# First two token tiles of a linear-attention and GEGLU block: order of loads, low words and products changed

## The chip, the cores and the metric

The kernel runs on one core of one Trainium2 chip. The metric is the device time of one execution in microseconds (us). The engines are named as in the profile: PE is TensorE (matrix products and transposes), DVE is VectorE, ACT is ScalarE, POOL is GpSimd, and SP is SyncE, whose queue issues the DMAs.

## The reference

2048 tokens of 576 features go through a layer norm; two branches read the result, and their product is added to the input. All arrays are float32.

```python
def _A_ref(x, wqkv, wo):                       # linear attention, 32 heads of 18
    qkv = ...(x @ wqkv).reshape(B, S, 3, H, Dh)
    phi = lambda t: jnp.where(t > 0, t + 1, jnp.exp(t)) + 1e-6
    pq, pk = phi(q), phi(k)
    kv = jnp.einsum("bhsd,bhse->bhde", pk, v)
    z = jnp.einsum("bhsd->bhd", pk)
    num = jnp.einsum("bhqd,bhde->bhqe", pq, kv)
    den = jnp.einsum("bhqd,bhd->bhq", pq, z)[..., None] + 1e-6
    return (num / den) ... @ wo

def _B_ref(x, w_gate, w_up, w_down):           # GEGLU
    h = gelu(x @ w_gate) * (x @ w_up)
    return h @ w_down

xn = _layernorm(x)
return x + _A_ref(xn, A_wqkv, A_wo) * silu(_B_ref(xn, ...))
```

## The kernel before

The 2048 tokens are cut into 16 tiles of 128. The first stage, the only one that the change touches, takes each tile through the layer norm and multiplies it with the k and v columns of `wqkv` (with a last group of q columns beside them). Later stages (the other q columns, the attention output, the gate, up and down matrices) take most of the 1500 us and are the same in both kernels.

**Words.** A float32 operand is used as two words: a high word, which is a copy into the type fp32r, and a low word, the difference of the source and the high word. Each product of x and W is seven passes over pairs of words (`KV_PASSES`, pairs of W word and x word). For one half j of the 576 features, x has a tile `xo` of five slots: 0 and 1 are the high words of two chunks of 128 features, 2 is a mixed slot that holds the last 32 features in several copies, partly as low words, and 3 and 4 are the low words of chunks 0 and 1. W has the same five slots. Pass (0, 3) needs x's low words, (3, 0) needs W's, and (2, 2) needs the mixed slot of both. `x_mm(t, c)` makes the product of tile t with column group c (0, 1, 2: 384, 384 and 448 columns), two halves of seven passes, 14 products in one PSUM bank.

**Preparing x.** `load_x` loads a tile, `spread` makes its mean and variance on DVE (two BN statistics, one aggregate) and the inverse root on ACT (Ln, Exp), `scales` mends it in three small DVE instructions, and `center` subtracts the mean and scales in place (one DVE instruction of 128x768). `turn` transposes the tile on PE in six pieces into two PSUM banks, three for each half j; `place` copies the high words out of PSUM (ACT, L85) and subtracts for the low words (DVE, two instructions a half: 128x256, and 32x128 for the mixed slot); `save` copies the float32 values out for later (ACT).

**Preparing W.** `load_kv(c, j)` loads one of six parts, `kv_hi` copies its high words (ACT), and `kv_lo(c, j, eng)` subtracts for its low words on the engine it is given: one instruction of 128x768 (896 for group 2) and one of 32x384 (448) for the mixed slot. Before, `kv_lo(0, 0)`, `kv_lo(1, 0)` and `kv_lo(2, 0)` run on DVE and `kv_lo(0, 1)`, `kv_lo(1, 1)`, `kv_lo(2, 1)` on POOL.

**After the products.** `k_post` applies phi to the k columns (two DVE instructions out of PSUM, Exp on ACT, an addition on POOL), `v_post` copies the v columns (ACT), `q_post` does phi for the q columns, ending with two POOL additions into `w_q`, and `kv_mm(t)` multiplies k with v into two PSUM banks. `q_turn` transposes `w_q` into a free corner of the x transposes' banks. `make_masks` fills constants with seven POOL instructions; they are read only after all tiles.

**Order.** Nearly every instruction is pinned to the program's order on its engine, and each engine works through its list in order; semaphores tie the engines together. The order of the first tiles is written out by hand at the end of `block_kernel`, from L1066 on: 22 transposes of a constant (`idle`, L1067) first, then the loads on SP's queue, then the preparations and products of tiles 0 to 2. From tile 3 on a loop calls `kv_tile`. The line numbers 85, 88, 91, 94 and 97 are the helpers that record each ACT, DVE, product, POOL and DMA instruction; L168 is the transpose in `turn`, L402 the one in `q_turn`. Transposed tiles 1 and later, and the product banks, share six PSUM banks (`bank`); tile 0's transposes use two others (`own_bank`).

Of the kernel before, what the change touches and what calls it, by code (L numbers as in the profile page):

```python
# [10 lines left out]
AF = mybir.ActivationFunctionType  # L11
# [42 lines left out]
def block_kernel(ctx, tc, x, xe, wq_d, wkv0_d, wkv1_d, wkv2_d, wo, wgu_d, wd_d, out):  # L54
# [6 lines left out]
    def bank(name):  # L61
        return ps.tile([P, 512], F32, tag="one", bufs=6, name=name)
# [21 lines left out]
    def act(*args, **kw):  # L84
        pin(nc.scalar.activation(*args, **kw))  # L85
# [4 lines left out]
    def mm(*args, **kw):  # L90
        pin(nc.tensor.matmul(*args, **kw))  # L91

    def pool(op, *args, **kw):
        pin(getattr(nc.gpsimd, op)(*args, **kw))  # L94
# [21 lines left out]
    def load_x(n, k):  # L116

        if n % 2 == 0:
            xstat[n // 2] = big(14 + n // 2 % 2, [P, 2, 2, 3 * P], F32, f"x_{n}")
        dma(  # L120
            out=xstat[n // 2][:, n % 2 : n % 2 + k],
            in_=xe[n * P : (n + k) * P].rearrange("(t p) j d -> p t j d", p=P),
        )
# [31 lines left out]
    def center(n):  # L155

        xs = xstat[n // 2][:, n % 2]
        m, r = scale_of.pop(n)
        vec("tensor_scalar", xs, xs, m, r, op0=ALU.subtract, op1=ALU.mult)

    def turn(n, new=bank):

        xs = xstat[n // 2][:, n % 2]
        tiles = [new(f"xt_{n}_{j}") for j in range(2)]
        xts[n] = [t[:, 0 : 3 * P].rearrange("p (k t) -> p k t", k=3) for t in tiles]
        for j in range(2):
            for k in range(3):
                pin(nc.tensor.transpose(xts[n][j][:, k, :], xs[:, j, k * P : (k + 1) * P], ident))  # L168
        q_turn([t for t in sorted(pqt) if t < n - 1], [(t, 3) for t in tiles])

    def place(n, js=(0, 1), words=(0, 1)):

# [16 lines left out]
    def save(n):  # L189

        tb, t = divmod(n, TT)
        s, b = divmod(tb, 2)
        for j, nm in enumerate(BS[b]):
            if t == 0:
                at_ = XM[s][nm]
                xf[s][nm] = (mid if at_ < 3 else big)(at_, [P, 3, TBN], F32, f"xf_{s}_{nm}")
            act(xf[s][nm][:, :, t * P : (t + 1) * P], xts[n][j], AF.Copy)
        xts.pop(n)

    mom, scale_of, xts = {}, {}, {}  # L200

    def to_operand(o, src, c):
        act(o[:, 0:3, c], src[:, :, c], AF.Copy)
# [15 lines left out]
    def keep(s, nm, o):  # L219
        d = dr.tile([P, 5, TBN], F32, name=f"kept_{s}_{nm}")  # L220
        dma(out=d, in_=o.bitcast(F32))
        store[s, nm] = d
# [24 lines left out]
    def kv_part(c, j, i):  # L247
        n = KV.index((c, j))
        if n < 5:
            return kv_parts(n, i, i + 1)[:, 0]  # L250
        w = 5 * CW[KV[i][0]]
        return wkv[i][:, w : w + CW[2]]
# [3 lines left out]
    def load_kv(c, j):  # L256
        n = KV.index((c, j))
        if n % 2 == 0:
            raws["kv", n // 2] = big((2, 3, 12)[n // 2], [P, 2, 3, CW[c]], F32, f"rw_{n}")
        raws[c, j] = raws["kv", n // 2][:, n % 2]  # L260
        dma(out=raws[c, j], in_=wkv_d[c][j])

    def kv_hi(c, j):
        n = KV.index((c, j))
        if n < 5:
            act(kv_parts(n, 0, 3), raws[c, j], AF.Copy)
        else:
            for i in range(3):
                act(kv_part(c, j, i), raws[c, j][:, i, :], AF.Copy)

    def kv_lo(c, j, eng, mixed=(False, True)):

        n, raw, r = KV.index((c, j)), raws[c, j], slice(2 * KR, 3 * KR)
        if False in mixed:
            if n < 5:
                eng("tensor_sub", kv_parts(n, 3, 5), raw[:, 0:2, :], kv_parts(n, 0, 2).bitcast(F32))
            else:
                for i in range(2):
                    eng(
                        "tensor_sub", kv_part(c, j, 3 + i), raw[:, i, :],  # L280
                        kv_part(c, j, i).bitcast(F32),
                    )
        if True in mixed:
            o = kv_part(c, j, 2)[r]
            eng("tensor_sub", o, raw[r, 2, :], o.bitcast(F32))
# [49 lines left out]


    KV_PASSES = [(0, 0), (1, 1), (3, 0), (4, 1), (0, 3), (1, 4), (2, 2)]
    pkv, pks, vas, es, pqt, pqx, ph4, ph, ph_d = ({} for _ in range(9))

    def x_mm(t, c):  # L340

        tb, i = divmod(t, TT)
        s, b = divmod(tb, 2)
        pkv[t, c] = o = bank(f"kv_{t}_{c}")
        for j in range(2):
            for n, (wi, xi) in enumerate(KV_PASSES):
                mm(
                    o[:, 0 : CW[c]], xo[s][BS[b][j]][:, xi, i * P : (i + 1) * P], kv_part(c, j, wi),
                    start=(j == 0 and n == 0), stop=(j == 1 and n == len(KV_PASSES) - 1),
                )  # L350

    def k_post(t, c):

# [13 lines left out]
    def v_post(t, c):  # L367

        if c == 1:
            vas[t] = slot([P, NHG, P], F32, f"va_{t}")  # L370
            pool("memset", vas[t][:, :, 0:1], 1.0)
        va, src = vas[t], pkv[t, c]
        n = 2 * TW - D
        if c == 1:
            src = src[:, TW - n : TW]
            act(va[:, 0, 1 : GW + 1], src[:, 0:GW], AF.Copy)
            act(va[:, 1, 1 : n - GW + 1], src[:, GW:n], AF.Copy)
        else:
            a = 2 * GW - n
            act(va[:, 1, n - GW + 1 : GW + 1], src[:, 0:a], AF.Copy)  # L380
            act(
                va[:, 2:4, 1 : GW + 1],
                src[:, a : a + 2 * GW].rearrange("p (g j) -> p g j", g=2), AF.Copy,
            )
            act(va[:, 4, 1 : W4 + 1], src[:, a + 2 * GW : TW], AF.Copy)

    def q_post(t):

        w = tmp([P, 4, Q4], f"w_q{t}")
        src, o, e = pkv[t, 2][:, TW : CW[2]], w[:, 2], w[:, 3]  # L390
        vec("tensor_scalar", e, src, 0.0, None, op0=ALU.min)
        vec("tensor_scalar", o, src, 0.0, EPS, op0=ALU.max, op1=ALU.add)
        act(e, e, AF.Exp)
        for i in range(2):
            pool("tensor_add", w[:, i], o, e)
        pqt[t] = w[:, 0:2]

    def q_turn(ts, banks):

        for t, (b, i) in zip(ts, banks):  # L400
            o = b[:, i * P : (i + 1) * P]
            pin(nc.tensor.transpose(o, pqt.pop(t), ident))  # L402
            pqx[t] = o

    def q_keep():
# [14 lines left out]
    def kv_tile(t, mid_=(), end=(), after=()):  # L420

        ahead = t % (2 * TT) != 2 * TT - 1
        x_mm(t, 0)
        if ahead:
            turn(t + 1)
        k_post(t, 0)
        x_mm(t, 1)
        if ahead:
            place(t + 1)
            save(t + 1)  # L430
        run(list(mid_))
        k_post(t, 1)
        v_post(t, 1)
        x_mm(t, 2)
        if t - 1 in vas:
            kv_mm(t - 1)
        run(list(end))
        v_post(t, 2)
        q_post(t)
        run(list(after))  # L440

# [625 lines left out]
        pin(nc.tensor.transpose(first[i % 2][:, 0:P], ident, ident))  # L1067
    load_x(0, 1)
    load_kv(0, 0)
    load_kv(0, 1)  # L1070
    load_x(1, 1)
    load_kv(1, 0)
    load_kv(1, 1)
    load_x(2, 1)
# [6 lines left out]
    center(0)  # L1081
    turn(0, own_bank)
    kv_hi(0, 0)
    kv_lo(0, 0, vec, (False,))
    place(0, (0,))
    kv_lo(0, 0, vec, (True,))
    kv_hi(0, 1)
    kv_lo(0, 1, pool)
    place(0, (1,), (0,))
    spread(1, 1)  # L1090
    kv_hi(1, 0)
    place(0, (1,), (1,))
    x_mm(0, 0)
    scales(1)
    center(1)
    kv_lo(1, 0, vec, (False,))
    kv_hi(1, 1)
    kv_lo(1, 1, pool)
    turn(1)
    place(1)  # L1100
    kv_lo(1, 0, vec, (True,))
    load_x(4, 2)
    x_mm(1, 0)
    kv_hi(2, 0)
    spread(2, 2)
    kv_lo(2, 0, vec)
    x_mm(0, 1)
    kv_hi(2, 1)
    kv_lo(2, 1, pool)
    save(0)  # L1110
    save(1)
    k_post(0, 0)
    x_mm(1, 1)
    scales(2)
    center(2)
    k_post(1, 0)
# [2 lines left out]
    x_mm(0, 2)  # L1119
    turn(2)  # L1120
    place(2)
    k_post(1, 1)
    v_post(1, 1)
    x_mm(1, 2)
    save(2)
    q_post(0)
    v_post(0, 2)
    center(3)
    q_post(1)
    v_post(1, 2)  # L1130
    make_masks()

    def x_next(n):

# [4 lines left out]


    x_mm(2, 0)
    kv_mm(0)
    turn(3)
    k_post(2, 0)
    x_mm(2, 1)
    place(3)
# [5 lines left out]
    kv_mm(1)  # L1152
    x_next(4)
    v_post(2, 2)
    q_post(2)
    load_q(0)
    for n in range(3, 2 * TT):
        ends = []
        if n < 2 * TT - 2:
            ends.append(lambda n=n: x_next(n + 2))  # L1160
        if n >= TT:
            j, c = divmod(n - TT, 2)
            prep_q(c, j)
            if n == TT + 1:
                load_q(1)
        if n == 2 * TT - 1:
            ends += [lambda i=i: difference(0, i) for i in range(3)]
        kv_tile(n, end=ends)
        if n in (4, 6):
            load_x(n + 4, 2)  # L1170
        if n == TT:
            for nm in BS[0]:
                keep(0, nm, xo[0][nm])
        if n == TT + 3:
            keep(0, "B22", xo[0]["B22"])

# [162 lines left out]
```

## Time and profile before

| | |
|---|---|
| median of 3 runs | 1501.02 us (1500.9 to 1503.89) |
| the profiled execution: its time | 1501.39 us |
| its span in the trace | 1499.7 us |
| PE busy in the span | 1489.9 us, 99% |
| DVE, ACT, POOL busy | 1063.7, 562.1, 537.2 us |
| tiles 0 to 3 (span 0 to 41.3 us) | the only part of the program with a changed order |

Times inside the trace count from the start of the span. A row of the timeline gives the start, the time to the last end, the engine, the line, the operation, output and inputs, the shape, the number of instructions merged, and in brackets the idle time before it with what ended that. A row of the table by windows gives, for each stretch, the busy time of each engine, the granted TensorE clock (1.00 is full), the busy share of the DMA engines and the GB/s they moved. Busy PE is modelled from pipelined products, so losses on PE are better read from the starts of its products.

### The profile page before, as it was taken

What the parts mean: (1) busy time and instruction counts of PE and PEld (TensorE: products, weight loads), DVE (VectorE), ACT (ScalarE), POOL (GpSimd) and SP (SyncE); (2) the same over time, 40 slices, a digit from 0 to 9 for tenths busy, and PEclk for the clock granted to TensorE, in tenths of its full rate; (3) what the DMA queues carried; (4) which work ended last, traced back from release to release, by engine and by line L of the source; (5) the groups of instructions that cost most, each with busy time, mean ns of one, the idle gap of its engine ahead of it and who ended that gap; (6) DMA issues with size and microseconds to landing.
All of it is one profiled execution on the core that took longest, in us unless ns stands there. A gap on an engine that the chain in (4) does not pass through costs nothing.

```text
span 1499.7 us, 22460 instructions
## 1 busy us (share of the span) xinstructions
PE 1489.9 (99%) x8390; PEld 1330.9 (89%) x8390; DVE 1063.7 (71%) x1604; ACT 562.1 (37%) x1047; POOL 537.2 (36%) x519
## 2 busy tenths in 40 slices
PE   8999999999999999999999999999999999999998
PEld 7989989988888888888888888888899999999998
DVE  7576476467887877788877788787785466555766
ACT  5435345333322233232232232222445454444443
POOL 4342340135655545655544665544410020000120
PEclk9999999999999999999999999999999999999999
DMA  4423204544444333443423443423688766786873
GB/s 185 142 119 136 83 3 182 182 189 157 172 155 152 120 128 134 172 173 135 152 106 128 167 172 146 160 111 128 213 321 264 232 211 227 232 283 226 292 253 116
DMA packets 112215, 257.15 MB, mean 171 GB/s; under 512 B 10138, under 2 KB 38682, under 8 KB 110058
## 3 DMA queue, kind: packets, MB, share of 16 engines
q1 hardware_dynamic: 110474, 246.80, 46.3%
q0 software_dynamic: 1632, 8.91, 1.6%
q8 instruction: 66, 1.08, 0.3%
q14 instruction: 43, 0.35, 0.1%
HBM read 157.73 MB, written 97.91 MB: 170 GB/s over the span
## 4 chain that ended last, share of the span: by engine, by line
PE 97%; DVE 1%; DMA 0%; POOL 0%; ACT 0%; issue 0%; SPq 0%; POOLq 0%; ACTq 0%
PE bd L952 26%; PE al L746 15%; PE de L746 15%; PE ga L746 15%; PE kv L91 8%; PE be L746 8%; PE s L91 4%; PE q L91 3%; PE kv_a L91 1%; PE xt L168 1%; DMA tr<-in_wd_dram 0%; PE idle L1067 0%; PE d L91 0%; PE kw L91 0%; PE b L91 0%
## 5 line engine op out<-in xcount | busy, mean ns | idle before, releaser
L952 PE MATMUL bd<-t,s 128*128 128x288 f32 x3024 | 401.3, 295 | 0.2 <-DVE u L88 0.2
L952 PEld LDWEIGHTS bd<-t,s 128*128 128x128 f32 x3024 | 400.9, 188 | 0.6 <-DVE u L88 0.5
L88 DVE TENSOR_TENSOR s<-sr,s 128x512 fp32r<-128x512 f32 x252 | 176.0, 738 | 120.0 <-ACT s L85 112.9
L85 ACT ACTIVATE s<-sr 128x512 fp32r<-128x512 f32 x252 | 148.9, 625 | 189.0 <-PE bd L952 128.1
L94 POOL TENSOR_TENSOR hs<-h,h 128x512 f32<-128x512 f32 x68 | 94.7, 1402 | 201.8 <-DVE h L88 199.1
L85 ACT ACTIVATE h<-h 128x512 f32<-128x512 f32 x108 | 67.0, 633 | 244.7 <-POOL sm L94 124.3
L94 POOL TENSOR_TENSOR sx<-sx 128x288 f32<-128x288 f32 x24 | 27.9, 1181 | 322.9 <-DVE sx L88 321.8
L91 PE MATMUL kv<-wkv,xo_B 128*128 128x384 f32 (+1 forms) x672 | 133.3, 353 | 1.3 <-POOL wkv L94 0.9
L91 PEld LDWEIGHTS kv<-wkv,xo_B 128*128 128x128 f32 x672 | 120.0, 190 | 6.8 <-POOL wkv L94 1.6
L88 DVE TENSOR_TENSOR wa<-raw,wa 128x256 fp32r<-128x256 f32 x72 | 81.2, 1128 | 49.6 <-ACT wa L85 46.4
L94 POOL TENSOR_TENSOR sm<-raw 128x384 f32<-128x384 f32 x72 | 75.7, 1051 | 110.3 <-DMA raw<-in_wgu_dram 70.8
L88 DVE TENSOR_TENSOR h<-h,u 128x512 f32<-128x512 f32 x108 | 95.7, 886 | 3.7
L85 ACT ACTIVATE wa<-sm 128x1152 fp32r<-128x1152 f32 x36 | 41.8, 1161 | 136.8 <-PE de L746 136.8
L88 DVE TENSOR_TENSOR wa<-sm,wa 128x768 fp32r<-128x768 f32 x72 | 63.4, 881 | 36.9 <-ACT wa L85 36.1
L94 POOL TENSOR_TENSOR td<-td 128x288 f32<-128x288 f32 x72 | 71.3, 991 | 50.6 <-DMA td<-in_wd_dram 46.4
L88 DVE TENSOR_TENSOR wb<-raw,wb 128x256 fp32r<-128x256 f32 (+1 forms) x108 | 72.4, 671 | 7.5 <-ACT wb L85 6.0
L88 DVE TENSOR_TENSOR wb<-sm,wb 128x256 fp32r<-128x256 f32 x72 | 60.9, 845 | 20.6 <-ACT wb L85 20.0
L85 ACT ACTIVATE u<-al 128x512 f32<-128x512 f32 x72 | 40.9, 592 | 88.1 <-PE al L746 88.1
L746 PE MATMUL al<-xo_B,wa 128*128 128x512 f32 x252 | 63.0, 389 | 0.0
L746 PE MATMUL al<-xr_B,wa 128*128 128x512 f32 x252 | 63.0, 389 | 0.0
L746 PE MATMUL be<-xo_T,wa 128*128 128x512 f32 x252 | 63.0, 389 | 0.0
L746 PE MATMUL be<-xr_T,wa 128*128 128x512 f32 x252 | 63.0, 389 | 0.0
(168 smaller groups left out, 2763.4 us busy)
## 6 DMA issues: line engine op xcount, KB each, us to landing
sr<-hs SPq DMA_DIRECT2D x252, 256.0 KB
hs<-h SPq DMA_DIRECT2D x68, 512.0 KB
raw<-in_wgu_dram SPq DMA_DIRECT2D x36, 768.0 KB
hs<-hs SPq DMA_DIRECT2D x102, 256.0 KB
td<-in_wd_dram SPq DMA_DIRECT2D x18, 576.0 KB
td<-td SPq DMA_DIRECT2D x18, 576.0 KB
tr<-td SPq DMA_DIRECT2D x16, 576.0 KB
tr<-in_wd_dram SPq DMA_DIRECT2D x12, 576.0 KB
```

The source lines that it names most:

```text
L85: pin(nc.scalar.activation(*args, **kw))
L88: pin(getattr(nc.vector, op)(*args, **kw))
L91: pin(nc.tensor.matmul(*args, **kw))
L94: pin(getattr(nc.gpsimd, op)(*args, **kw))
L168: pin(nc.tensor.transpose(xts[n][j][:, k, :], xs[:, j, k * P : (k + 1) * P], ident))
L746: nc.tensor.matmul(o, w[0:rows, wi, :], xop[0:rows, xi, :], start=(start and n == 0), stop=(n == len(PASSES) - 1), skip_group_check=True,)
L952: nc.tensor.matmul(banks[j][:, 0:HALF], hw[n, s][:, a, t * P : (t + 1) * P], w[:, c, g % 4], start=(new and g == 0 and m == 0), stop=(g == ...
```

## The change

Six things change, all in the first tiles:

- On SP's queue tile 1's load moves ahead of the second part of W's group 0.
- `kv_lo(0, 0)` moves from DVE to POOL. POOL then makes three of the first four parts' low words; `kv_lo(1, 0)` stays on DVE and is one piece, behind tile 1's low words.
- Tile 1's statistics and centring stand ahead of W's second part on ACT and DVE; tile 1's transposes stand in the midst of tile 0's first product.
- `x_mm` takes a list of passes, so that the products with W's high words (`HI`) of both tiles run first, and those with its low words (`LO`) and the mixed slots (`MIX`) of the second half come behind them, in turn for tiles 0 and 1.
- `q_post` is parted: its DVE instructions (`q_parts`) come earlier in the hand-written order. Tile 3's transposes stand ahead of `kv_mm(0)`, and only tile 0's `w_q` is transposed there; tile 1's follows with tile 2's, one tile later.
- `make_masks` is called after tile 5 in the loop.

```diff
-    def turn(n, new=bank):
+    def turn(n, new=bank, q=True):
...
-        q_turn([t for t in sorted(pqt) if t < n - 1], [(t, 3) for t in tiles])
+        if q:
+            q_turn([t for t in sorted(pqt) if t < n - 1], [(t, 3) for t in tiles])
+        else:
+            xtb[n] = tiles
...
     KV_PASSES = [(0, 0), (1, 1), (3, 0), (4, 1), (0, 3), (1, 4), (2, 2)]
+    HI, LO, MIX = [(0, 0), (1, 1), (0, 3), (1, 4)], [(3, 0), (4, 1)], [(2, 2)]
+    def of(*jp):
+        return [(j, p) for j, ps_ in jp for p in ps_]
...
-    def x_mm(t, c):
+    def x_mm(t, c, passes=None):
...
+        for j, (wi, xi) in passes or [(j, p) for j in range(2) for p in KV_PASSES]:
+            n = left[t, c] = left[t, c] - 1
+            mm(
+                pkv[t, c][:, 0 : CW[c]], xo[s][BS[b][j]][:, xi, i * P : (i + 1) * P],
+                kv_part(c, j, wi), start=(n == 2 * len(KV_PASSES) - 1), stop=(n == 0),
+            )
...
     load_kv(0, 0)
+    load_x(1, 1)
     load_kv(0, 1)
-    load_x(1, 1)
...
     kv_hi(0, 0)
-    kv_lo(0, 0, vec, (False,))
-    place(0, (0,))
-    kv_lo(0, 0, vec, (True,))
-    kv_hi(0, 1)
-    kv_lo(0, 1, pool)
-    place(0, (1,), (0,))
+    kv_lo(0, 0, pool)
+    place(0, (0, 1), (0,))
     spread(1, 1)
-    kv_hi(1, 0)
-    place(0, (1,), (1,))
-    x_mm(0, 0)
+    place(0, (0,), (1,))
     scales(1)
     center(1)
-    kv_lo(1, 0, vec, (False,))
+    kv_hi(0, 1)
+    x_mm(0, 0, of((0, HI), (0, LO), (0, MIX), (1, HI[:2])))
+    place(0, (1,), (1,))
+    kv_lo(0, 1, pool)
+    turn(1)
+    place(1, (0, 1), (0,))
+    x_mm(0, 0, of((1, HI[2:])))
+    kv_hi(1, 0)
+    place(1, (0, 1), (1,))
+    x_mm(1, 0, of((0, HI[:2]), (0, LO), (1, HI[:2]), (0, HI[2:]), (0, MIX), (1, HI[2:])))
+    kv_lo(1, 0, vec)
     kv_hi(1, 1)
     kv_lo(1, 1, pool)
-    turn(1)
-    place(1)
-    kv_lo(1, 0, vec, (True,))
+    x_mm(0, 0, of((1, LO), (1, MIX)))
+    x_mm(1, 0, of((1, LO), (1, MIX)))
     load_x(4, 2)
-    x_mm(1, 0)
+    x_mm(0, 1, of((0, HI), (0, LO), (0, MIX), (1, HI)))
+    x_mm(1, 1, of((0, HI), (0, LO), (0, MIX), (1, HI)))
     kv_hi(2, 0)
+    save(1)
     spread(2, 2)
     kv_lo(2, 0, vec)
-    x_mm(0, 1)
+    x_mm(0, 1, of((1, LO), (1, MIX)))
     kv_hi(2, 1)
     kv_lo(2, 1, pool)
     save(0)
-    save(1)
     k_post(0, 0)
-    x_mm(1, 1)
+    x_mm(1, 1, of((1, LO), (1, MIX)))
...
-    make_masks()
...
     x_mm(2, 0)
+    turn(3, q=False)
     kv_mm(0)
-    turn(3)
+    q_turn((0,), [(xtb.pop(3)[0], 3)])
...
+        if n == TT + 1:
+            make_masks()
```

More of the change, by code (lines that the diff above doesn't have):

```diff
@@ L193, in save @@
         for j, nm in enumerate(BS[b]):
-            if t == 0:
+            if nm not in xf[s]:
                 at_ = XM[s][nm]
@@ L198, in save @@
         xts.pop(n)
-    mom, scale_of, xts = {}, {}, {}
+    mom, scale_of, xts, xtb = {}, {}, {}, {}
     def to_operand(o, src, c):
@@ L337, in block_kernel @@
     KV_PASSES = [(0, 0), (1, 1), (3, 0), (4, 1), (0, 3), (1, 4), (2, 2)]
+    HI, LO, MIX = [(0, 0), (1, 1), (0, 3), (1, 4)], [(3, 0), (4, 1)], [(2, 2)]
+    def of(*jp):
+        return [(j, p) for j, ps_ in jp for p in ps_]
+    left = {}
     pkv, pks, vas, es, pqt, pqx, ph4, ph, ph_d = ({} for _ in range(9))
-    def x_mm(t, c):
+    def x_mm(t, c, passes=None):
         tb, i = divmod(t, TT)
         s, b = divmod(tb, 2)
[L344 to L350, printed above, removed]
+        if (t, c) not in pkv:
+            pkv[t, c] = bank(f"kv_{t}_{c}")
+            left[t, c] = 2 * len(KV_PASSES)
+        for j, (wi, xi) in passes or [(j, p) for j in range(2) for p in KV_PASSES]:
[4 more added lines that the diff above has]
+            )
     def k_post(t, c):
@@ L385, in v_post, with q_parts @@
             act(va[:, 4, 1 : W4 + 1], src[:, a + 2 * GW : TW], AF.Copy)
-    def q_post(t):
+    def q_parts(t):
         w = tmp([P, 4, Q4], f"w_q{t}")
@@ L392, in q_post @@
         vec("tensor_scalar", o, src, 0.0, EPS, op0=ALU.max, op1=ALU.add)
-        act(e, e, AF.Exp)
+        pqt[t] = w
+    def q_post(t):
+        w = pqt[t]
+        act(w[:, 3], w[:, 3], AF.Exp)
         for i in range(2):
-            pool("tensor_add", w[:, i], o, e)
-        pqt[t] = w[:, 0:2]
+            pool("tensor_add", w[:, i], w[:, 2], w[:, 3])
     def q_turn(ts, banks):
@@ L401, in q_turn @@
             o = b[:, i * P : (i + 1) * P]
-            pin(nc.tensor.transpose(o, pqt.pop(t), ident))
+            pin(nc.tensor.transpose(o, pqt.pop(t)[:, 0:2], ident))
             pqx[t] = o
@@ L438, in kv_tile @@
         v_post(t, 2)
+        q_parts(t)
         q_post(t)
@@ L1121, in block_kernel @@
     place(2)
-    k_post(1, 1)
     v_post(1, 1)
-    x_mm(1, 2)
-    save(2)
-    q_post(0)
     v_post(0, 2)
     center(3)
+    k_post(1, 1)
+    q_parts(0)
+    x_mm(1, 2)
+    q_post(0)
+    save(2)
+    q_parts(1)
+    v_post(1, 2)
     q_post(1)
-    v_post(1, 2)
-    make_masks()
     def x_next(n):
@@ L1154, in block_kernel @@
     v_post(2, 2)
+    q_parts(2)
     q_post(2)
```

## Prediction

> **What bounds the kernel now.** I read the page first: which engine is full, and which carries the chain that ended last.
>
> ```profile
> PE 1489.9 (99%) x8390; PEld 1330.9 (89%) x8390; DVE 1063.7 (71%) x1604; ACT 562.1 (37%) x1047; POOL 537.2 (36%) x519
> ...
> PE 97%; DVE 1%; DMA 0%; POOL 0%; ACT 0%; issue 0%; SPq 0%; POOLq 0%; ACTq 0%
> ```
>
> PE sets the end. A change of order is worth what it takes from PE's lost time, and only the first 41 us are reordered. So I read PE's timeline there.
>
> ```profile
> 8.16 2.12 PE L91 MATMUL kv<-wkv,xo_B 128*128 128x384 f32 x9 [0.25 <-ACT xo_B L85]
> 11.18 1.53 PE L91 MATMUL kv<-wkv,xo_B 128*128 128x384 f32 x5 [0.89 <-POOL wkv L94]
> 13.02 1.15 PE L168 MATMUL xt<-ident,x 128*128 128x128 f32 x6 [0.31 <-DVE x L88]
> 14.14 11.98 PE L91 MATMUL kv<-wkv,xo_B 128*128 128x384 f32 x56
> ...
> 34.16 0.33 PE L402 MATMUL xt<-ident,w_q 128*128 128x128 f32 x1 [0.41 <-POOL w_q L94]
> 34.85 0.33 PE L402 MATMUL xt<-ident,w_q 128*128 128x128 f32 x1 [0.36 <-POOL w_q L94]
> 34.93 5.59 PE L91 MATMUL kv<-wkv,xo_B 128*128 128x384 f32 x28
> ```
>
> PE waits for POOL's low words, for tile 1's centring on DVE, and for POOL's `w_q`. The 56 products took 11.98 us where a full-rate pitch of 0.173 us (384 columns, later tiles) gives 9.7. The table by windows says why.
>
> ```profile
> 14.00:15.00 1.00, 1.00 (x4) 0.86 (x4) 0.81 (x3) 0.88 (x3) 1.00 (x1) 0.50 1.05 436
> 15.00:16.00 1.00, 1.00 (x5) 1.00 (x4) 0.94 (x3) 0.91 (x1) 0.92 (x2) 0.50 0.77 225
> ...
> 17.00:18.00 1.00, 1.00 (x8) 1.00 (x7) 0.94 (x4) 0.00 (x0) 0.00 (x0) 1.00 0.87 338
> ```
>
> The granted clock is 0.50 from 13.48 to 16.89, after a stretch in which PE stood still for half the time.
>
> **PE's lost time before**, from the starts of single products (gap less the pitch: 0.173 us at 384 columns, 0.207 at 448, 0.109 for a transpose), from 7.06, tile 0's transposes, to 41.34, tile 3's first product: tile 0's first copy 0.55; low words of W's first part 0.28; POOL's low words of W's second part 1.16 and its mixed slot 0.26; tile 1's centring 0.64; its copy 0.39; half clock 1.34; group 2's low words 0.30; the two `w_q` transposes 1.15; small gaps 0.1. Sum **6.2 us**; the other 28.1 us are work, which the change keeps.
>
> **The change, walked through with these durations.** I lay the changed instructions engine by engine in their built order and let each start when its engine and its inputs are ready. The same walk on the old order puts tile 2's transposes at 25.7 (measured 25.97) and tile 4's first product 0.4 early, so I trust differences to some 0.4 us.
>
> *Loads.* The trace's record of landings (last of 16 parts) has tile 0 at 3.78, W's first part 5.15, its second 7.73, tile 1 8.73. The second part lagged: most of it landed by 6.5, its last piece 1.2 later. Tile 1 in that place, 384 KB for 576, would be mostly in by 6.05, and with the same lag at 7.3; W's second part then lands at 8.73, since the bytes ahead of it are the same, and so do all later loads. SP issues each load in 0.4 to 0.5 us, all of them by 6.2, ahead of their landings, so the swap in its queue costs nothing itself. If the lag goes, tile 1 gains at most until DVE is free at 6.9; if it falls on tile 1 alone, it lands as before, 8.73. I take 7.3.
>
> *Tile 1's chain.* Before it ran from its first BN statistic to its centring without foreign waits, with two low-word instructions in it, as it will now:
>
> ```profile
> 8.89 0.55 DVE L88 TENSOR_TENSOR wkv<-rw,wkv 32x384 fp32r<-32x384 f32 x1
> 9.47 0.82 DVE L88 BATCH_NORM_STATS2 bn<-x 128x6 f32<-128x288 f32 x2
> ...
> 12.28 0.68 DVE L88 TENSOR_SCALAR x<-x,mv,st 128x768 f32<-128x768 f32 x1
> ...
> 15.67 1.34 DVE L88 TENSOR_TENSOR wkv<-rw,wkv 32x384 fp32r<-32x384 f32 x1
> ```
>
> So 12.28-9.47 = 2.81 us: centring from 10.11 to 10.79, transposes at 10.89 in place of 13.02. PE is free for them at 10.4.
>
> *First low words on POOL.* DVE loses 0.95+0.55 us ahead of tile 1, which is what lets the chain start on landing. On POOL they start at 6.63, after ACT's copy; POOL's 128x768 takes 1.88 us and its 32x384 1.00 (rows at 9.25 and 11.21), the first being held until tile 0's centring ends at 6.96: ready at 8.65 and 9.73. The passes that need them come fifth and seventh, at 9.4 and 9.8: hidden to 0.1. Without this cover each us late costs one, until PE's wait for tile 1 (0.45) is used up.
>
> *Added wait.* Tile 0's low x words now stand behind tile 1's statistics on DVE: 7.3+1.29 = 8.58 to 9.0, where PE wants them at 8.6: 0.5 lost with the restart. Behind that product wait only tile 0's others; ACT's and DVE's queues go on.
>
> *ACT.* W's second part is copied from 8.84 (behind tile 1's Exp, 1.54 us after its first statistic) to 9.99: 0.1 lost. Group 1's copies move behind tile 1's, to 12.1-14.3; the products that read them start at 14.9. Its low words on DVE (13.4-14.9) are wanted at 15.6, on POOL (to 17.7) at 18.7. W's second part's low words (POOL, 10.8-13.5) are wanted at 13.9. These covers are 0.4 to 1 us.
>
> *Half clock.* From 10.9 PE hardly stops, so I drop the 1.34. By busy pitches, 1.6 of the 3.41 us before 13.48 were enough to lose the clock and 2.35 of the 3.41 before that kept it; the walk gives 2.25 and 3.0. [...] A halved clock in either window would cost 0.5 by the walk, as it eats the wait below; in both 1.7.
>
> *Tile 2's centring* is late next. DVE takes up group 2's low words at 17.1, is held twice by POOL's, and centres tile 2 at 22.6-23.25; PE has finished at 22.6 and stands 0.8 until 23.4, and 0.3 for the copies. If DVE's small instruction gets ahead of POOL's last one, this wait goes (gain 1.1 more); if it is held once more, 1.1 is added.
>
> *Masks and `w_q`.* The seven POOL instructions (1.75 us) ahead of the `w_q` additions go: 1.15 back. In tile 5 POOL idles 1.45 and 1.39 us in the rows around them, which hides them; uncovered they would cost 1.75 less that. Tile 1's transpose moves one tile on: nothing in sum.
>
> **Lost after:** 0.55 + 0.5 + 0.1 + 0.1 + 0.45 (tile 1) + 0.15 + 0.8 + 0.3 = 2.95, or 2.9 by the walk. **Gain 3.3 us.** Later stages are PE's chain, so it carries to the end: 1501.39 - 3.3 = 1498.1 for the profiled execution, which stood 0.37 over the median; against the median **1497.7 us**.
>
> **Rivals.** *The port is lost* (0.24). DVE and POOL do not run two-input work side by side: the DVE rows above show 32x384 at 0.55 alone and 1.34 beside POOL, and POOL's addition below took 1.73 beside a centring and 1.42 without.
>
> ```profile
> 30.06 0.68 DVE L88 TENSOR_SCALAR x<-x,mv,st 128x768 f32<-128x768 f32 x1
> ```
> ```profile
> 30.30 1.73 POOL L94 TENSOR_TENSOR pk<-pk,e_k 128x576 f32<-128x576 f32 x1 [1.78 <-ACT e_k L85]
> ...
> 38.89 1.42 POOL L94 TENSOR_TENSOR pk<-pk,e_k 128x576 f32<-128x576 f32 x1 [4.09 <-ACT e_k L85]
> ```
>
> In the new order tile 1's centring (10.11) meets POOL's 128x768 for W's second part: ACT's copy ends 2.69 us after the first statistic, and POOL started 0.08 or 0.13 after such ends (9.17 to 9.25; 13.22 to 13.35), so at 10.07-10.12. It is a tie. POOL's list has three waits there, as at 13.35, so I take 0.13, and DVE first by 10 ns. If POOL is first, centring ends at 12.5: transposes 1.7 later, PE under half busy from 10.06, half clock again (1.3), less tile 2's 0.8: gain 1.1, **1499.9**. [...]
>
> *Tile 1 lands late, and the port is lost* (0.05), the slower side: tile 1 in at 8.73 as before, transposes at 14.0, five products of tile 0 still behind them: 0.5 slower, **1501.5**. It decides from a landing of about 8.3.
>
> *The early gain is hidden behind tile 2* (0.09): DVE held once more ahead of tile 2's centring; the rows at 15.67 speak for it, as does POOL's earlier start. Gain 2.2, **1498.8**.
>
> **Numbers.** The forecast has 0.57; its own range is gains of 2.5 to 4.1. A measurement can tell about 0.2%, 3.0 us. Some three quarters of the forecast's chance lie beyond that, 0.44, and 0.02 of tile 2's case: faster 0.46. The rest of both, the lost port and the late tile (0.5 slower is within) make 0.49. For slower by 3 us no row speaks; the 0.05 left is for what the trace can't show, a new wait in the 1460 us after. The range runs from 1496.6 (gain 4.1 with some jitter) to 1500.6, a lost port with tile 1 landing 0.7 late.
>
> **What would show it.** Right: tile 1's transposes near 10.9, no clock of 0.50, no POOL row before the `w_q` transpose, tile 3's first product near 38.0. Wrong: centring of tile 1 at 1.7 or more us in place of 0.68; an idle PE before 23 that names POOL; tile 1's statistics at 8.8.

## The result and the profile after

The changed kernel takes **1498.01 us** in the middle of 8 runs (1497.31 to 1499.4) where the kernel before took 1500.96 (8 runs, 1500.69 to 1503.89): ratio 0.9978, 95% interval 0.9968 to 0.9987. So it is faster by 0.22%; the forecast was 1497.7 us. The profiled execution is the longest of the eight, 1499.4 us with a span of 1497.7. Its page, engines and chain:

```profile
PE 1488.4 (99%) x8390; PEld 1330.9 (89%) x8390; DVE 1062.0 (71%) x1602; ACT 561.9 (38%) x1047; POOL 541.2 (36%) x521
...
PE 98%; DVE 1%; DMA 0%; issue 0%; ACT 0%; SPq 0%; ACTq 0%
```

PE still sets the end, and POOL has left the chain. PE's timeline after:

```profile
7.10 0.85 PE L168 MATMUL xt<-ident,x 128*128 128x128 f32 x6 [0.60 <-PE idle L1084]
8.20 0.62 PE L91 MATMUL kv<-wkv,xo_B 128*128 128x384 f32 x2 [0.25 <-ACT xo_B L85]
9.89 2.61 PE L91 MATMUL kv<-wkv,xo_B 128*128 128x384 f32 x7 [1.08 <-DVE xo_B L88]
12.30 1.15 PE L168 MATMUL xt<-ident,x 128*128 128x128 f32 x6
13.21 11.66 PE L91 MATMUL kv<-wkv,xo_B 128*128 128x384 f32 x61
25.37 0.85 PE L168 MATMUL xt<-ident,x 128*128 128x128 f32 x6 [0.50 <-PE kv L91]
...
33.35 0.29 PE L418 MATMUL xt<-ident,w_q 128*128 128x128 f32 x1
...
39.78 2.52 PE L91 MATMUL kv<-wkv,xo_B 128*128 128x384 f32 x13
```

(L1084 and L418 are here what L1067 and L402 were before.) Tile 1's transposes come at 12.30 (13.02 before), tile 3's first product at 39.78 (41.34 before). The `w_q` transpose waits for nothing, and no wait names POOL's low words. New are a wait of 1.08 us for tile 0's low x words (0.5 forecast) and, as forecast, about 0.8 us without work ahead of tile 2's transposes (24.40 to 25.37, less one product). PE's lost time by the forecast's ledger is 4.7 us (6.2 before, 2.95 forecast). The table by windows, same columns as before, shows a half clock that the forecast did not have:

```profile
8.00:9.00 1.00, 0.62 (x2) 0.30 (x2) 0.74 (x2) 0.53 (x2) 0.92 (x2) 1.00 0.98 387
9.00:10.00 1.00, 0.11 (x1) 0.11 (x1) 0.90 (x5) 0.61 (x3) 0.73 (x1) 0.78 1.03 404
10.00:11.00 1.00, 1.00 (x3) 1.00 (x4) 0.86 (x5) 0.94 (x1) 0.00 (x0) 0.50 1.03 412
```

DVE's timeline says what the head waited for:

```profile
8.26 0.82 DVE L88 BATCH_NORM_STATS2 bn<-x 128x6 f32<-128x288 f32 x2 [1.26 <-DMA x<-in_xe_dram]
...
10.93 0.68 DVE L88 TENSOR_SCALAR x<-x,mv,st 128x768 f32<-128x768 f32 x1
```

Tile 1's last piece landed at 8.23, not at 7.3; DVE stood idle for 1.26 us. So this one execution misses the forecast's details, while the median meets its total. The experiments ask what belongs to the program and what to the execution.

### The profile page after: what moved, and what is told of

The parts are those of the page before. It is cut to its first block, busy times and chain, and to the rows that moved or that the text cites. A ratio compares the mean times of both kernels' runs of the same rounds, so it can differ in the third digit from the quotient of the medians.

```text
span 1497.7 us, 22459 instructions
## 1 busy us (share of the span) xinstructions
PE 1488.4 (99%) x8390; PEld 1330.9 (89%) x8390; DVE 1062.0 (71%) x1602; ACT 561.9 (38%) x1047; POOL 541.2 (36%) x521
## 3 DMA queue, kind: packets, MB, share of 16 engines
q8 instruction: 66, 1.08, 0.3%
## 4 chain that ended last, share of the span: by engine, by line
PE 98%; DVE 1%; DMA 0%; issue 0%; ACT 0%; SPq 0%; ACTq 0%
PE bd L969 27%; PE al L763 15%; PE de L763 15%; PE ga L763 15%; PE kv L91 8%; PE be L763 8%; PE s L91 4%; PE q L91 3%; PE kv_a L91 1%; PE xt L168 1%; DMA x<-in_xe_dram 0%; PE d L91 0%; PE kw L91 0%; PE b L91 0%; DVE sx L88 0%
## 5 line engine op out<-in xcount | busy, mean ns | idle before, releaser
L763 PE MATMUL ga<-xo_T,wa 128*128 128x512 f32 x252 | 63.0, 389 | 0.0
```

What stands on the lines that cost most here:

```text
L763: nc.tensor.matmul(o, w[0:rows, wi, :], xop[0:rows, xi, :], start=(start and n == 0), stop=(n == len(PASSES) - 1), skip_group_check=True,)
```

## The experiments

One table carries most of the reading, a row for each profiled execution: tile 1's last piece landed (the trace's record of landings); centring of tile 1, start and length, and how long behind its start POOL's subtraction started; tile 1's first transpose T1; tile 3's first product T3; the time of that execution; and the median of all runs of the kernel (us). T1 and T3 come from the starts of single instructions.

| kernel | landed | centring | POOL behind | T1 | T3 | T3-T1 | time | median |
|---|---|---|---|---|---|---|---|---|
| before | 8.73 | 12.28, 0.68 | 1.06 | 13.02 | 41.34 | 28.32 | 1501.39 | 1500.96 |
| after | 8.23 | 10.93, 0.68 | 0.135 | 12.30 | 39.78 | 27.48 | 1499.40 | 1498.01 |
| after again | 8.00 | 10.70, 0.68 | 0.139 | 11.44 | 38.66 | 27.23 | 1498.22 | 1497.53 |
| masks only | 9.03 | 12.15, 0.68 | 1.07 | 12.89 | 40.02 | 27.14 | 1499.51 | 1499.71 |
| old load order | 8.56 | 11.26, 0.68 | 0.137 | 11.99 | 39.49 | 27.50 | 1499.07 | 1500.07 |
| old load order again | 9.01 | 11.71, 0.68 | 0.136 | 13.08 | 40.74 | 27.66 | 1500.37 | 1499.58 |
| centring late | 6.73 | 9.80, 0.68 | 0.214 | 10.56 | 37.74 | 27.18 | 1497.33 | 1497.78 |
| centring later | 6.85 | 10.55, 2.07 | -0.157 | 12.67 | 39.88 | 27.21 | 1499.46 | 1499.71 |
| x first | 5.14 | 10.10, 1.45 | 0.037 | 11.81 | 38.95 | 27.14 | 1498.48 | 1500.64 |
| low words on DVE | 7.16 | 11.65, 2.31 | 0.087 | 14.01 | 42.27 | 28.26 | 1501.80 | 1500.83 |
| tile 2 centred early | 6.98 | 9.70, 0.68 | 0.405 | 10.48 | 38.41 | 27.93 | 1497.94 | 1498.18 |
| scale in another form | 7.74 | 10.44, 0.68 | 0.139 | 11.18 | 38.39 | 27.21 | 1497.96 | 1497.65 |
| ... and mixed slot late | 7.50 | 9.94, 0.68 | 0.405 | 10.72 | 37.90 | 27.18 | 1497.48 | 1497.38 |
| scales of one tile, mixed slot late | 7.62 | 10.06, 0.68 | 0.406 | 10.84 | 38.11 | 27.27 | 1497.67 | 1497.67 |

Two constants stand out. The time less T3 is 1459.5 to 1459.6 us in every row but the first (1460.05). And T3-T1 is 27.1 to 27.3, save where half clock, the masks or a new wait lengthen it. Almost everything, then, is decided by T1.

**The changed kernel again**, unedited.

> The changed kernel once more, nothing edited: it shows which of its lost times belong to the program and which to one execution. My theory: the gain is the masks' 1.15 us plus what the head saves, and the head's saving depends on two things that may vary from execution to execution, when tile 1 lands (8.23 us in the profile after, 7.3 in my forecast) and whether the half clock comes (9.56 to 12.98 us in the profile after). So: about 1497.3 to 1498.4 us as the other runs of it; in the profile tile 3's first product lies at 38.3 to 39.8 us (39.78 before), nearer 38.4 if the window of half clock is missing. Rival: all of it belongs to the program; then tile 1 lands at 8.2, the half clock lies at the same place, and the first product of tile 3 at 39.8 within 0.1 us.

1497.53 us (11 runs), ratio 0.9976 (0.9967 to 0.9985). T3 is at 38.66, 1.1 earlier than in the first profile, though tile 1 landed only 0.23 earlier. The rest is the clock, which this table by windows shows at 1.00 throughout:

```profile
9.00:10.00 1.00, 0.37 (x3) 0.34 (x3) 0.90 (x5) 0.84 (x3) 0.68 (x1) 1.00 1.07 419
10.00:11.00 1.00, 1.00 (x6) 0.72 (x5) 0.89 (x4) 0.71 (x1) 0.16 (x1) 1.00 1.00 402
```

In two profiles with half clock ahead of T1 (after; old load order again) the transposes began 0.69 us after the end of the centring, as PE still had products to do; in the other rows 0.05 to 0.11, but for x first (0.27, where PE waited for POOL's low words). So the half clock cost the first profile 0.6 us at T1 and 0.3 behind it. It belongs to the execution, and so does the landing: in the nine profiled executions with the changed kernel's order of loads tile 1 lands at 6.73 to 8.23, the middle one at 7.50, and two of them (after; low words on DVE) have half clock.

**Masks only**: the kernel before with `make_masks` after tile 5.

```diff
-    make_masks()
...
+        if n == TT + 1:
+            make_masks()
```

> The kernel before with only the masks moved to after tile 5. My theory (the masks are one term of 1.15 us, the reordered head is the rest): 1.15 us under the kernel before, about 1499.8 us; the two w_q transposes no longer wait for POOL, tile 3's first product lies near 40.2 us where it was 41.34, and the half clock stays where it was (13.5 to 16.9 us). Rival A (the head's reordering brought nothing, the masks all): 1498.0 us, as fast as the changed kernel. Rival B (what is saved at the w_q transposes is given back by the seven POOL instructions in tile 5): 1501.0 us, with a new wait of PE for POOL around tile 5.

1499.71 us beside 1500.89 for the kernel before, measured with it: 1.18 us, the term of 1.15. The ratio alone, 0.9994 (0.9985 to 1.0003), could not show it; what shows it is T3-T1, 27.14 for 28.32. This execution had no half clock, and its PE timeline tells what the half clock was worth in the kernel before:

```profile
12.89 0.87 PE L168 MATMUL xt<-ident,x 128*128 128x128 f32 x6 [0.17 <-DVE x L88]
14.01 7.55 PE L91 MATMUL kv<-wkv,xo_B 128*128 128x384 f32 x42 [0.25 <-ACT xo_B L85]
22.91 3.13 PE L91 MATMUL kv<-wkv,xo_B 128*128 128x448 f32 x14 [1.34 <-DVE pk L88]
25.87 0.82 PE L168 MATMUL xt<-ident,x 128*128 128x128 f32 x6
```

PE runs the products at full rate, and then stands 1.34 us for the bank that `k_post` frees on DVE. Tile 2's transposes come at 25.87, where half clock had them at 25.97. Before the change the half clock was hidden: DVE paced this stretch.

**The old order of loads**, twice, all else as changed.

```diff
-    load_x(1, 1)
     load_kv(0, 1)
+    load_x(1, 1)
```

> The changed kernel with one edit: tile 1's load stands behind the second part of W's group 0 again, as in the kernel before; all other reordering stays. My theory, since tile 1 lagged in the profile after (8.23 us against 8.73 us in the old order): the new place of the load is worth only 0.5 us or less of landing, so this kernel is 0 to 0.6 us slower than the changed one, and W's second part, landing at 7.7 instead of 9.7, gives nothing. Rival (the place of the load is what the head's gain stands on, as my walk had it with a landing at 7.3): 1.4 us slower, 1499.4 us, and tile 1's transposes near 13.8 us where they were at 12.3.

> The changed kernel with the old order of loads once more, unedited. Its first run gave 1500.07 us in the middle, 2.1 to 2.5 above the changed kernel, while the one profiled execution took 1499.07 and shows tile 1 landing at 8.56 us, the centring unheld (POOL 0.137 us behind it) and half clock, so what makes the usual execution another 1.0 us longer is open. Theory A (the port: the usual execution has POOL ahead at tile 1's centring, 1.8 to 2.4 us instead of 0.68): the profile shows a centring of 1.8 us or more and tile 1's transposes near 13.5. Theory B (a later landing, 8.9 us or more) shows tile 1's statistics at 8.9 or later with a centring of 0.68. Theory C (half clock costs more in the usual execution): two windows of 0.50. If the profile falls again on an execution of 1499 us, it stays open.

1500.07 and 1499.58 us, ratios 0.9992 (0.9983 to 1.0001) and 0.9987 (0.9978 to 0.9996): some 2 us over the changed kernel, so my theory (0.6 at most) fell. It had taken 8.23, the latest landing of the new order, for the usual one. Tile 1 lands at 8.56 and 9.01 here against 7.50 in the middle, and both profiles have half clock around PE's wait for it. The rival's 1.4 was too small as well. The second profile shows theories B and C together: tile 1's statistics at 9.04, and two windows of half clock (9.84 to 16.67). Theory A's centring of 1.8 us or more is not there:

```profile
9.04 0.82 DVE L88 BATCH_NORM_STATS2 bn<-x 128x6 f32<-128x288 f32 x2 [2.07 <-DMA x<-in_xe_dram]
...
11.71 0.68 DVE L88 TENSOR_SCALAR x<-x,mv,st 128x768 f32<-128x768 f32 x1
```

**Centring late and later**: one, then three small DVE instructions ahead of tile 1's centring, so that POOL's subtraction might start first.

```diff
     scales(1)
+    c_ = scale_of[1][1]
+    for _ in range(3):
+        vec("tensor_scalar", c_, c_, 1.0, None, op0=ALU.mult)
     center(1)
```

> The changed kernel with one small extra DVE instruction ahead of tile 1's centring (it multiplies one 128x1 scale by 1.0, so the values stay). In the profile after the centring started at 10.933 us and POOL's 128x768 subtraction of W's second part would have been free to start at 11.07, 0.13 behind it: a lead of 0.13 us. The extra instruction takes 0.06 to 0.25 us. [...] Rival (the two run side by side, and the order of the two does not matter): centring 0.7 us long, transposes 0.1 to 0.25 later, and no change in time that can be told.

> The run with one small extra DVE instruction did not decide it: POOL's 128x768 subtraction of W's second part still came 0.21 us behind the centring, as tile 1 had landed at 6.73 us and DVE's lead was larger. Here three such instructions, 0.25 us from start to start each, stand ahead of tile 1's centring, 0.75 us in all, more than the largest lead seen (0.21+0.25 = 0.46 us). Nothing else differs from the changed kernel. [...] Rival (side by side): the centring lasts 0.7 us, the transposes come 0.75 us later than they would, and the time is 0 to 0.75 us above.

One instruction left the order as it was (1497.78 us, ratio 0.9982, 0.9973 to 0.9991): with a landing at 6.73 DVE's lead was still 0.21. Two of its eleven executions took 1500.09 and 1501.16, with a mean granted clock of 0.998 and 0.997; their traces were not had. The profile comes closest to the forecast's case: T1 at 10.56 (forecast 10.9), T3 at 37.74 (38.0). With three, POOL was first:

```profile
10.55 2.07 DVE L88 TENSOR_SCALAR x<-x,mv,st 128x768 f32<-128x768 f32 x1
```
```profile
10.39 3.07 POOL L94 TENSOR_TENSOR wkv<-rw,wkv 128x768 fp32r<-128x768 f32 x2 [0.36 <-POOL wkv L94]
```

The centring took 2.07 us for 0.68, and the kernel 1499.71 us (ratio 0.9991, 0.9982 to 1.0001), 1.7 to 2.2 over the changed one. By the forecast of that run 0.75 of it is the added instructions; the longer centring is 1.39. Nothing was taken back from tile 2's wait, which stands at 0.77 as in both profiles of the changed kernel: T3-T1 is 27.21.

**Low words of W's first part on DVE.**

```diff
-    kv_lo(0, 0, pool)
+    kv_lo(0, 0, vec)
```

> The changed kernel with the low words of W's first part back on DVE, as one edit. My theory (the move to POOL is worth only what DVE would else wait for it when tile 1 has landed): on DVE they take 0.95+0.55 us from about 6.95, to 8.5 us; tile 1's statistics start at 8.5 where they started on landing, 6.8 to 8.26; so 0.3 us later with a late landing and 1.7 later with an early one: 0.2 to 1.2 us above the changed kernel. For it speaks also that tile 0's low x words come later on DVE. Rival (the move is what frees DVE and is the larger part of the head's gain of 1.9 us): 1.5 us or more above the changed kernel in all executions. Second rival (POOL's instructions of 1.99 and 0.99 us are slower than DVE's, so the product with W's low words comes earlier on DVE): as fast or faster.

1500.83 us, ratio 0.9999 (0.9991 to 1.0008): the whole gain is gone, as the first rival had it. DVE's and POOL's rows show two losses:

```profile
7.44 1.52 DVE L88 TENSOR_TENSOR wkv<-rw,wkv 128x768 fp32r<-128x768 f32 x2
8.97 0.82 DVE L88 BATCH_NORM_STATS2 bn<-x 128x6 f32<-128x288 f32 x2
...
11.65 2.31 DVE L88 TENSOR_SCALAR x<-x,mv,st 128x768 f32<-128x768 f32 x1
```
```profile
11.73 3.08 POOL L94 TENSOR_TENSOR wkv<-rw,wkv 128x768 fp32r<-128x768 f32 x2 [10.03 <-ACT wkv L85]
```

Tile 1 was there at 7.16; its statistics waited until 8.97. And the centring took 2.31 us for 0.68, although POOL's record starts 0.087 us after its own. POOL, without work until then, started 0.083 us after ACT's copy ended (11.650), where it took 0.131 in the runs that had given it the first low words. The second loss I had not expected. Half clock came on top (12.50 to 19.33, T3-T1 28.26 for 27.2). This was the longest of the eleven executions, so it is not shown that the usual one has the long centring too; the shortest took 1500.25.

**Tile 1 ahead of all of W.**

```diff
     load_x(0, 1)
-    load_kv(0, 0)
     load_x(1, 1)
+    load_kv(0, 0)
```

> The changed kernel with tile 1's load in front of W's first part as well: tile 0, tile 1, W's first part, its second. Over the profiles so far the last piece of tile 1 landed at 6.73, 8.00 and 8.23 us in the new order, while the second load, W's first part, landed complete at 5.13 to 5.7 in all. My theory (tile 1's late pieces set the head): tile 1 lands by 5.2 us, its statistics follow tile 0's centring at 6.9 us, its centring lies at 9.5 to 9.9 us, and POOL's low words of W's first part come later, as ACT's copy of it waits for a landing of 6 to 8 us; tile 3's first product at 37.5 to 38.5 us in each execution, 1497.1 to 1498.0 us, and a narrower spread than the changed kernel's 1497.2 to 1499.4. Rival (W's first part then lags instead, as third load): first product of tile 0 later than 8.2 to 8.4 us, up to 10, and 0 to 1.5 us above the changed kernel.

1500.64 us, ratio 0.9995 (0.9986 to 1.0004). Tile 1 landed at 5.14 and W's first part at 6.95, but its copy and POOL's subtraction (8.22) moved back too, and POOL's next one came 0.037 us behind the centring, which took 1.45 us for 0.68. That execution took 1498.48; nine of the eleven took 1500.3 to 1501.0, beyond what both theory and rival allowed. Their traces were not had, but their record has a mean granted clock of 0.997 or 0.998 where the two short ones have 1.000, and one window of half clock takes 0.001 off it (half of 3.41 us in 1500). So half clock goes with the long ones; what brings it is open.

**Three tries at tile 2's wait.** The first centres tile 2 ahead of group 2's low words; the second gives its multiplication of 1.00 to 1.02 us another form, and a copy of that kernel also puts tile 0's 32x128 low words behind tile 1's centring and the product that reads them behind tile 1's transposes; the third has that last edit, and works out tile 2's scales alone, in 128x1 instructions.

```diff
+    scales(2)
+    center(2)
     kv_lo(2, 0, vec)
...
-    scales(2)
-    center(2)
...
-    x_mm(0, 2)
+    x_mm(0, 2, of((0, HI), (1, HI), (0, LO), (1, LO), (0, MIX), (1, MIX)))
```

> The changed kernel with tile 2's scales and centring ahead of DVE's low words of W's first part of group 2, and tile 0's product with group 2 in the order high words first. It aims at the wait that stands in three of three profiles of the changed head: PE idle 0.77 us ahead of tile 2's transposes, 0.2 and 0.1 us for the copies after. My theory (DVE's queue, in which the low words of group 2 beside POOL take 2.5 us ahead of that centring, makes the wait): the wait goes, tile 3's first product comes 0.6 to 1.0 us earlier at the same landing, about 1497.0 us, 0.6 to 1.0 us under the changed kernel. Rival (DVE's work is the bound to 25 us whatever its order, so the wait moves to the low words of group 2 or to the banks that k_post frees): no gain, 0 to 0.5 us either way.

```diff
-            vec("tensor_mul", c, c, v)
+            vec("scalar_tensor_tensor", c, c, 1.0, v, op0=ALU.mult, op1=ALU.mult)
```

> The changed kernel with one edit: the multiplication of two 128x2 scales, a TENSOR_TENSOR that took 1.00 to 1.02 us ahead of tile 2's centring in every profile where POOL's 32x448 subtraction had started 0.17 to 0.19 us before it, and 0.161 us in the one where it ran ahead of POOL, becomes a SCALAR_TENSOR_TENSOR of the same value (times 1.0). Two instructions of that form took 0.160 to 0.163 us next to it, but none of them started well inside a POOL instruction, so it is not shown that the form is free of the wait. My theory (that instruction is held by POOL and the form is not): tile 2's centring comes 0.84 us earlier, PE's wait of 0.77 us ahead of its transposes goes to 0.1 or less, tile 3's first product comes 26.4 to 26.6 us after tile 1's first transpose where it came 27.2, and the time is 0.7 us under the changed kernel, about 1497.0 us. Rival A (the form is held too): no change. Rival B (as with the earlier centring of tile 2: the wait moves to the banks that k_post frees): 0 to 0.3 us.

> The edit of the run before, and tile 0's 32x128 low words put behind tile 1's centring, with the two products that need them behind tile 1's transposes. DVE's chain to that centring loses 0.28 us of low words; in a late landing, where the chain waits for them (scales started 0.03 us after they ended and 0.30 after ACT's Exp), the centring comes 0.25 us earlier against ACT's copy of W's second part, so POOL's subtraction starts 0.38 us behind it where it was 0.135 to 0.139. My theory (centring starts decide the head, and a centring with POOL 0.087 us or less behind it was held while one with 0.135 was not): 0.25 us under the run before or the same, with the port never lost, so no execution above about 1498.5 but by half clock. Rival (DVE's total work from tile 1 to tile 2 is the bound, so moving 0.28 us behind the centring gives nothing): equal to the run before within 0.1 us.

```diff
-    scales(2)
+    scales(2, 0)
     center(2)
+    scales(2, 1)
```

> The edit with tile 0's 32x128 low words behind tile 1's centring, and another one for tile 2's scales (without the SCALAR_TENSOR_TENSOR of before, which was held for 1.00 us like the multiplication it replaced): they are worked out for one tile at a time, three TENSOR_SCALAR of 128x1 ahead of tile 2's centring and three for tile 3 behind it. In this case's traces a TENSOR_SCALAR of 128x1 took 0.15 to 0.22 us also where POOL's subtraction was under way (0.154 us at 9.35 us in the profile after, 0.215 at 9.11 in the run with one small instruction), while those of 128x2 there took 0.76 us and 1.00. My theory (only the 128x2 forms and the centring wait for POOL): the three take 0.75 us where it was 1.43, tile 2's centring starts inside POOL's last 32x448 subtraction and ends 0.42 us after it, 0.5 us earlier against tile 1's than before, PE's wait ahead of tile 2's transposes falls from 0.78 to about 0.3 us, tile 3's first product comes 26.7 us after tile 1's first transpose where it came 27.2, and the time is 1496.9 us, 0.5 under the run with the same first edit. Rival (the wait is the banks that k_post frees, or tile 2's copies): the same time as that run.

1498.18 (ratio 0.9982, 0.9973 to 0.9991), 1497.65 (0.9976, 0.9966 to 0.9985), 1497.38 (0.9975, 0.9965 to 0.9985) and 1497.67 us (0.9978, 0.9969 to 0.9987). None can be told from the changed kernel by its median. In the first, the second and the last a rival was right; in the third the theory was. There the centring started 2.44 us after the landing instead of 2.70, POOL's subtraction 0.405 behind it (0.38 forecast), and T3-T1 stayed at 27.18: the 0.28 us moved behind the centring went into 0.39 us that DVE had stood idle there, waiting for ACT. The median is 0.27 lower (0.25 forecast). The other form of the scale took just as long (1.012 us where the old one took 1.016). Tile 2 centred early cost 0.7 us of T3-T1 in waits for group 2's low words and `k_post`'s banks. The last shortened tile 2's wait as it set out to, and PE's timeline shows where it went:

```profile
22.13 0.83 DVE L88 TENSOR_SCALAR x<-x,mv,st 128x768 f32<-128x768 f32 x1
22.88 0.70 DVE L88 TENSOR_SCALAR st<-st 128x1 f32<-128x1 f32 x3
23.49 0.55 DVE L88 TENSOR_SCALAR e_k<-kv 128x384 f32<-128x384 f32 x1
23.95 0.55 DVE L88 TENSOR_SCALAR pk<-kv 128x384 f32<-128x384 f32 x1
```
```profile
23.06 0.85 PE L176 MATMUL xt<-ident,x 128*128 128x128 f32 x6
24.56 5.56 PE L91 MATMUL kv<-wkv,xo_B 128*128 128x448 f32 x28 [0.66 <-DVE pk L88]
```

The transposes come 12.22 us after T1 instead of 12.8, with 0.26 us lost ahead of them instead of 0.77; then the next product waits for `k_post(1, 0)` (`pk`, to 24.50). From T1 to the end of that instruction DVE takes 13.64 us in the changed kernel's second profile and 13.67 here. As far as this pair shows, the length of DVE's list, with what is longer in it beside POOL, paces PE from tile 1 to tile 2, and not the place of one wait in it.

## Why the prediction was right, and where its steps were not

The total was right, 1497.7 for 1498.0 and 1497.5, and so was the mechanism at its end: an earlier tile 1, and no POOL ahead of `w_q`. Step by step:

- *Masks, 1.15 us.* Right: 1.18 by the masks alone.
- *The rest of the gain.* The forecast summed PE's lost times and counted **1.34 us for the half clock that goes**. This step failed. That time was DVE's already: without half clock, masks only lost some 5.05 us in PE's ledger, which is 6.2 less 1.15, the 1.34 having turned into a wait for a bank. What paid is T1: 13.02 before, 11.2 to 11.4 after at a landing of 7.7 to 8.0, so 1.6 to 1.8 us, with the same 27.2 behind it. With 1.15 that makes 2.8 to 3.0. T1 came 3.44 us after the landing in both, so at the middle landing of 7.50 I estimate T1 at 10.9 and 3.2 in sum. The medians differ by 2.95 and, measured again, by 3.4. The sum came out because the walk also put 0.8 and 0.3 us on tile 2, DVE's price in PE's terms.
- *Tile 1 lands at 7.3.* 7.50 in the middle of nine executions, 8.23 in the one first seen. The old order gave 8.56 to 9.03, so 1.1 to 1.5 us later, and some 2 us of time with the clock.
- *Added wait for tile 0's low words, 0.5.* 1.25 and 0.79 lost in the two profiles of the changed kernel, where tile 1 landed at 8.23 and 8.00. In the execution without half clock it did not delay T1, which followed the centring by 0.06.
- *Low words on POOL.* Ready at 8.67 and 9.73 (forecast 8.65 and 9.73). Where tile 1 landed at 6.73 (centring late) PE did stand 0.42 us for them, though T1 still followed the centring by 0.08. Undoing the move takes the whole gain; in the profiled execution the centring also took 2.31 us for 0.68.
- *The port.* What the forecast calls so, its rows show in lengths alone: DVE's 32x384 at 0.55 and 1.34 us, POOL's addition at 1.42 and 1.73; what ties the two engines no run shows. DVE started first, as forecast, but not by the forecast's tie: from first statistic to centring it took 2.68 us, not 2.81, so POOL came 0.135 behind, not 0.01. At 0.037 and 0.087 the centring took 1.45 and 2.31 us, so by my estimate it would have been long at 0.01 too. No run shows the rival's centring that ends 2.4 us after POOL's start; with POOL first (centring later) it ended 2.23 after. That this run, with its added instructions, measured 1499.71 where the rival had 1499.9 is luck: the rival summed 1.7 for the transposes and 1.3 of half clock, less 0.8 from tile 2; the profile has 1.39 for the centring, no half clock, and nothing back from tile 2.
- *Tile 2's wait, 0.8.* Right, 0.77 in the profile after. That its removal would gain 1.1 more was wrong: one edit removed it, another cut it to 0.26, and neither gained.
- *Half clock.* It changes with the execution: after has it and after again has not; the first window on record begins at 6.15 in the profile after, at 6.65 in the one before. In one window it cost 0.9, for which the forecast had 0.5. The forecast had also misread PE's work ahead of it: counted as in the last section, 1.3 us in the window before 13.48, which half clock followed, and 2.2 in the one before that, which full clock followed, for its 1.6 and 2.35.
- *Later stages carry the difference to the end.* Right within 0.1 us between all profiles but before's. That one lost another 0.45 late, at the start of the down projection; the execution with the old head and late masks did not, and its cause is open.

Open too is why the last pieces of a load lag.

## What to carry to other kernels

Before lost times of the busiest engine are added up, ask which of them sit in a stretch that another engine paces: those turn into each other. A distance between two marks that stays fixed over several edits (here 27.2 us from tile 1's transposes to tile 3) says that none of them touched what paces the stretch, and leaves one number to work on; the waits inside it name the engine. Where an instruction was longer beside another engine's, as the centring here (0.68 us with a lead of 0.135 or more over POOL, 1.45 and 2.31 with 0.037 and 0.087), read the lead between their starts, and give the one on the critical path a few tenths rather than a few hundredths.

## What the runs showed of the hardware

- **Centring beside POOL's subtraction.** A centring whose record starts ahead of POOL's subtraction by 0.135 us or more ran in 0.68 us (table). Ahead by 0.037 (x first) or 0.087 (low words on DVE), one case of each, it took 1.45 and 2.31 us, though it started first by the records; 0.157 behind (centring later), 2.07. No case lies between 0.087 and 0.135. POOL's 128x768, started behind a centring, took 2.23 us in the profile after (11.07), and 1.88 in the one before at 9.25. Two long DVE instructions ended 0.42 us after POOL's: the 32x384 at 15.67 in the profile before (17.01; POOL's 16.59), and tile 2's centring in the run with scales of one tile (22.96; 22.54).
- **Small DVE instructions.** Inside a POOL subtraction, TENSOR_SCALAR of 128x1 took 0.15 us (after, at 9.35) to 0.22 (centring late, at 9.11), and of 128x2 0.76 (after, at 18.83), where one ahead of POOL took 0.17 (before, at 19.06); TENSOR_TENSOR and SCALAR_TENSOR_TENSOR of 128x2 took 1.00 to 1.02 (after, at 23.36; scale in another form).
- **The clock.** Half clock lasted 3.41 us in the profiles before (13.48 to 16.89) and after (9.56 to 12.97), and 6.83 in low words on DVE (12.50 to 19.33) and old load order again (9.84 to 16.67). I counted PE work (starts times pitch) in windows of 3.41 us laid off from these. At full clock, 1.0 us (old load order again, to 9.84), 1.1 (after, to 9.56) and 1.3 (before, to 13.48) were followed by half clock, and 2.2 (before, 6.65 to 10.06) by full clock. In a window at half clock some 2.5 us (old load order again, to 13.25) were followed by half clock once more, 3.2 (after) and 3.5 (before) by full clock. What decides it these profiles do not show.
- **A lagging piece.** Of the 16 pieces of tile 1's load, three came late in the profile after (7.00, 7.56 and 8.23 us, the rest by 6.27) and two in the one before (8.36 and 8.73, the rest by 7.94), and the lag stayed with the loads behind (last pieces at 8.23, 9.67 and 11.06 us in the profile after, where most were in by 6.3, 7.8 and 9.2).
